# The queue order of an FNet and H3 kernel, taken from another machine model in the scheduler

## Chip, cores and metric

One core of a Trainium2 chip runs the whole program in one launch. The metric is the device time of one execution in microseconds (us), median over runs; less is better. The profile is of one further execution.

## What is computed

Two mixing layers are applied in turn, twice: an FNet layer (A) and an H3 layer (B). S = 2048 positions, D = 576 channels, float32.

```python
def _A_ref(x, dft_seq_re, dft_seq_im, dft_hid_re, dft_hid_im):
    a = jnp.einsum("bsd,ed->bse", x, dft_hid_re)
    b = jnp.einsum("bsd,ed->bse", x, dft_hid_im)
    return jnp.einsum("ts,bse->bte", dft_seq_re, a) - jnp.einsum("ts,bse->bte", dft_seq_im, b)

def _B_ref(q, k, v, shift_k, ssm_k, ssm_D):
    ...                      # k_shift: causal convolution of k with 4 taps
    kv = k_shift * v
    ...                      # y: causal convolution of kv with ssm_k over all 2048 positions, by FFT
    y = y + kv * ssm_D[None, None, :]
    return q * y

x = x + _A_ref(_layernorm(x), ...)
x = x + _B_ref(_layernorm(x), B_k, B_v, ...)
x = x + _A_ref(_layernorm(x), ...)
x = x + _B_ref(_layernorm(x), B_k, B_v, ...)
```

The factor y of layer B does not depend on x, so it is computed once and used in both B layers.

## The kernel before

Every float32 operand of a matmul is held as two float32r parts, a high and a low one, and a product takes three matmuls (high x high, high x low, low x high). `split` (L72, L73) makes the parts: ACT copies the high part, DVE subtracts it to get the low one. All matmuls are issued by the helper at L58.

**The trunk** is the first A layer: the sequence transform of the normalised x, then the hidden transform. `layer` (L251) runs 128 steps: 4 blocks of output positions (tb), for each the real and then the imaginary matrix (g), for each 16 steps k over the positions that are summed. Here a *trunk block* is one (tb, g), 16 steps, numbered 0 to 7. Step k loads one 128 x 512 tile of coefficients (`load_c`, L172; rings of three buffers, craw and cs), splits it, and runs 14 matmuls: 12 into four accumulators s0 to s3 and 2 into rm, which holds the last 64 channels. At the block's end `evac_u` splits the four accumulators into U, and `evac_r` does the same for rm:

```python
    def evac_r(g, ps):
        ...
        tmp = work()[lo:lo + REM, :NT]
        nc.scalar.activation(tmp, ps[NC][other:other + REM], AF.Copy)
        nc.vector.tensor_tensor(tmp, tmp, ps[NC][lo:lo + REM], OP.add)
        split(u[:, 0, :], u[:, 1, :], tmp)
```

Those are L216 to L224, with L222 on ACT and L223 on DVE. There is one buffer each for s0 to s3, rm and U. After both blocks of a tb the hidden transform `hidden` (L226) runs 8 pieces of 27 matmuls each (`bk<-w,mats` in the profile), one piece at a time between trunk steps, and the first of them need the weights from `load_w`.

**The branch** (`branch`, from L296) computes y of layer B with an FFT in three stages, written into the program between the trunk steps, with counts that set how many of its pieces stand ahead of which step (L538 to L546):

- The first stage (`f1_loads`, `f1_split`, `f1_products`; `bk<-f1r`): 32 units of 12 matmuls. A unit of v takes eight DVE operations (L347, L349, L350) for the 4 taps and the product with v. Results go to DRAM from ACT's queue (L364, L365).
- The middle stage (`mid_split`, `mid_forward`, `mid_inverse`; `bk<-mid`): 64 groups. A group reads one tile back from DRAM, splits it, runs 6 matmuls into two banks, copies (ACT, L399 to L402) and multiplies (DVE, L405 to L408), splits again, runs 3 matmuls into a third bank, and stores (L419, L420).
- The inverse stage (`i2_split`, `i2_products`; `bk<-i`): 16 pieces of 12 matmuls, which leave y in DRAM (yb).

The branch and the hidden transform share three PSUM banks (bk).

**The end of layer 1.** For each of 16 tiles, `get_x1` (L508) loads the result of the first A layer (xa) and yb, normalises and gates (`gated`, L474 and L475), stores, normalises again (`normed`, L148, L150), stores y for the second layer, and writes the split X tile (`to_x`, L155 to L158). The second A layer uses another algorithm (`strassen`) for three of its four tb and ends with 16 hidden tiles and gatings.

**Rings.** Scratch and landing buffers are slots cut out of a few large tiles, and a ring hands them out in the order in which the program is written. `work` (four slots, then three) serves the first and middle stage, the normalisations and evac_r alike; `land` (three or four) serves the loads of branch, weights, xa and yb; `res` (two) the x tiles. An operation that gets a slot waits until everything written earlier in the program is done with it.

**What sets the order.** The program is written as one sequence. A scheduler gives each of the five queues (TensorE, DVE, ACT, POOL, and SP, which issues most loads) its instructions in an order that it chooses: it runs the program on a model of the machine, and at each point takes, of the instructions that are ready there, the one that is earliest in the program. The order it finds is then fixed, and semaphore waits are put in. Loads of coefficients in the later part are held behind each other by `issue_after` (L126).

## Time and profile before

| | us |
|---|---|
| median of 3 runs | 1280.3 (1276.68 to 1282.56) |
| the profiled execution | 1286.63 |
| its span, first to last instruction | 1284.6 |
| granted TensorE clock, mean | 0.98 of full speed |

The span of the profiled execution falls into these parts. The times of the trunk blocks' ends are those of their last rm matmul.

| part | us from the start of the span |
|---|---|
| end of trunk blocks 0, 1, 2, 3 | 84.5, 166.5, 247.7, 360.3 |
| end of trunk blocks 4, 5, 6, 7 | 464.9, 543.1, 657.3, 718.8 |
| last matmul of the first stage of the branch | 218.5 |
| first gating of layer 1 (L475) | 674.3 |
| second layer's first rm matmul | 750.0 |
| last 16 hidden tiles | from about 1165 |

Busy time in some stretches of 40 us, us of 40:

| stretch | TensorE | DVE | ACT | GB/s |
|---|---|---|---|---|
| 0 to 40 | 29.39 | 26.60 | 24.69 | 300 |
| 200 to 240 | 36.26 | 20.52 | 25.57 | 231 |
| 440 to 480 | 38.51 | 34.72 | 34.89 | 150 |
| 720 to 760 | 28.78 | 28.93 | 12.43 | 187 |

In a line of the groups, after the shapes and the count come the busy time in us and the mean of one instruction in ns, then the idle time of the engine just before them and what ended most of it. In a line of the timeline stand the start, the duration, the engine and the line of the kernel, and in brackets the idle time before and what ended it. In the rows of tenths each digit is the busy share of one fortieth of the span, 32.1 us.

### The profile page before, as it was taken

Reading aid. Unit: us, or ns where it says so; the run is one execution under the profiler, and the core shown is the slowest. Engines: PE = TensorE matmul, PEld = TensorE weight load, DVE = VectorE, ACT = ScalarE, POOL = GpSimd, SP = SyncE. Lnnn points to the kernel's source line nnn. Section 1 sums busy time; section 2 is a strip of 40 time slices with the busy share of each in tenths; the row PEclk is TensorE's granted clock in tenths of the full one; section 3 lists DMA queues with packets and bytes.
Section 4 is the critical chain, followed back from the end, with each engine's and each line's share of the span. In section 5 each row is a group of like instructions: output and inputs, shape, how many; then the busy total and the mean of one; then the engine's idle time right before and its main releaser. Section 6 shows DMA issues by size and latency. Waiting matters only on the chain.

```text
span 1284.6 us, 18381 instructions
## 1 busy us (share of the span) xinstructions
PE 1210.3 (94%) x6320; PEld 1040.3 (81%) x6320; DVE 866.2 (67%) x1597; ACT 654.2 (51%) x1290; POOL 50.7 (4%) x68
## 2 busy tenths in 40 slices
PE   6799999799999999999999879899999999989998
PEld 5677888698889888789878768787878778779997
DVE  6788895737775697853358865565666657775764
ACT  5775675728865688854553332434443344451200
POOL 1100000000000000000002111000000000000111
PEclk9999999999999999999999989899999989999999
DMA  8968888635544555447878754774375467586642
GB/s 300 294 200 257 280 250 268 201 100 157 164 135 133 147 150 161 146 129 223 260 243 249 218 192 158 232 245 128 115 251 166 132 214 233 153 264 214 205 152 74
DMA packets 140367, 250.32 MB, mean 195 GB/s; under 512 B 15217, under 2 KB 39793, under 8 KB 140274
## 3 DMA queue, kind: packets, MB, share of 16 engines
q1 hardware_dynamic: 106290, 206.68, 52.5%
q10 hardware_dynamic: 33984, 42.48, 9.4%
q8 instruction: 49, 0.80, 0.3%
q14 instruction: 44, 0.36, 0.1%
HBM read 187.76 MB, written 61.34 MB: 194 GB/s over the span
## 4 chain that ended last, share of the span: by engine, by line
PE 53%; DMA 18%; DVE 11%; ACT 9%; issue 6%; POOL 1%; ACTq 0%; SPq 0%; POOLq 0%; DVEq 0%
PE s L58 27%; PE bk L58 23%; PE rm L58 4%; DMA flts<-vd 3%; DMA flts<-in_c_mat 3%; DVE mats L73 2%; DMA flts<-yb 2%; DMA flts<-in_x 2%; DMA t<-flts 1%; ACT mats L72 1%; DMA t<-f1f 1%; DMA flts<-xa 1%; DVE flts L408 1%; ACT flts L401 1%; DMA ud<-ph 1%
## 5 line engine op out<-in xcount | busy, mean ns | idle before, releaser
L58 PE MATMUL s<-mats 128*128 128x512 f32 x2292 | 583.2, 396 | 15.8 <-ACT mats L155 7.7
L58 PEld LDWEIGHTS s<-mats 128*128 128x128 f32 x2292 | 426.5, 190 | 103.1 <-ACT mats L155 10.0
L72 ACT ACTIVATE mats<-flts 128x512 fp32r<-128x512 f32 (+1 forms) x270 | 167.5, 626 | 180.3 <-PE rm L58 113.8
L73 DVE TENSOR_TENSOR mats<-flts,mats 128x512 fp32r<-128x512 f32 (+1 forms) x270 | 183.7, 686 | 81.8 <-ACT mats L72 80.0
L58 PE MATMUL bk<-w,mats 128*128 128x288 f32 x864 | 124.0, 299 | 4.8 <-DVE mats L73 3.0
L58 PEld LDWEIGHTS bk<-w,mats 128*128 128x128 f32 x864 | 119.9, 192 | 7.8 <-DVE mats L73 3.7
L58 PE MATMUL rm<-mats 128*128 128x512 f32 x338 | 107.0, 398 | 8.3 <-DVE flts L223 8.3
L58 PE MATMUL bk<-mid 128*128 128x288 f32 x576 | 97.6, 303 | 14.8 <-ACT mid L72 9.0
L58 PEld LDWEIGHTS bk<-mid 128*128 128x128 f32 x576 | 85.4, 189 | 30.8 <-ACT mid L72 12.4
L58 PE MATMUL s<-t,mats 128*128 128x512 f32 x384 | 99.1, 396 | 2.1 <-ACT ph L616 1.3
L72 ACT ACTIVATE mid<-flts 128x288 fp32r<-128x288 f32 (+1 forms) x128 | 71.7, 563 | 40.6 <-DVE flts L408 35.9
L58 PE MATMUL bk<-mats 128*128 128x288 f32 (+1 forms) x580 | 92.0, 304 | 0.0
L143 POOL TENSOR_TENSOR flts<-flts 128x1 f32<-128x1 f32 x56 | 43.2, 773 | 1199.4 <-DVE flts L142 1188.9
L58 PEld LDWEIGHTS s<-t,mats 128*128 128x128 f32 x384 | 73.1, 191 | 18.7 <-ACT ph L616 1.7
L72 ACT ACTIVATE t<-flts 128x512 fp32r<-128x512 f32 x78 | 48.6, 628 | 73.3 <-PE rm L58 19.4
L58 PEld LDWEIGHTS bk<-mats 128*128 128x128 f32 x580 | 82.3, 189 | 2.4
L73 DVE TENSOR_TENSOR mid<-flts,mid 128x576 fp32r<-128x576 f32 (+1 forms) x128 | 77.0, 606 | 9.2 <-ACT mid L72 5.3
L58 PEld LDWEIGHTS rm<-mats 128*128 128x128 f32 x338 | 64.2, 191 | 22.0 <-DVE flts L223 8.7
L73 DVE TENSOR_TENSOR t<-flts,t 128x512 fp32r<-128x512 f32 x78 | 53.3, 688 | 30.4 <-ACT t L72 30.1
L58 PE MATMUL bk<-f1r 128*128 128x288 f32 x384 | 63.8, 304 | 10.3 <-ACT f1r L72 7.0
L58 PEld LDWEIGHTS bk<-f1r 128*128 128x128 f32 x384 | 59.1, 194 | 17.1 <-ACT f1r L72 7.0
L238 DVE TENSOR_TENSOR flts<-flts,bk 128x288 f32<-128x288 f32 x56 | 25.2, 451 | 54.9 <-PE bk L58 54.6
(112 smaller groups left out, 1327.5 us busy)
## 6 DMA issues: line engine op xcount, KB each, us to landing
flts<-in_c_mat SPq DMA_DIRECT2D x84, 512.0 KB, 4.0
flts<-in_c_mat SPq DMA_DIRECT2D x160, 256.0 KB, 3.6
flts<-t SPq DMA_DIRECT2D x64, 288.0 KB, 2.9
t<-f1f ACTq DMA_DIRECT2D x42, 288.0 KB, 4.3
flts<-in_x SPq DMA_DIRECT2D x32, 288.0 KB, 4.0
vd<-flts ACTq DMA_DIRECT2D x64, 144.0 KB, 3.2
flts<-vd SPq DMA_DIRECT2D x32, 288.0 KB, 3.6
flts<-yb SPq DMA_DIRECT2D x32, 288.0 KB, 3.5
```

Of the source, the lines that this page charges most:

```text
L58: nc.tensor.matmul(ps, lhsT, rhs, start=first, stop=last, skip_group_check=more)
L72: nc.scalar.activation(h, src, AF.Copy)
L73: nc.vector.tensor_tensor(l, src, h.bitcast(F32), OP.subtract)
L143: nc.gpsimd.tensor_tensor(rs, ve, mhalf, OP.pow)
L238: nc.vector.tensor_tensor(xa[:, cs], r[:, cs], ps[:, :HD], OP.add)
L401: nc.scalar.activation(kk[lo, 1, :], pk[hi, :HD], AF.Copy)
L408: nc.vector.tensor_tensor(p1, p1, p2, OP.add)
```

## The change

The model of the machine on which the scheduler runs the program is exchanged: the default one for the scheduler's timeline model. The kernel function, its tiles, buffers and instructions stay as they are; only the order of each queue, and with it where the semaphore waits stand, comes out of another model.

```diff
     o = nc.dram_tensor("out_0", (P, J, D), F32, kind="ExternalOutput").ap()
-    with tile.TileContext(nc, auto_bufs=True) as tc:
+    with tile.TileContext(nc, auto_bufs=True, schedule_with_timeline_sim=True) as tc:
         fnet_h3_kernel(tc, **args, out=o)
```

Of the queues of the built program, 4367 of TensorE's 6322 instructions stand at another place than before (42 places on average over the queue, 261 at most), 1197 of DVE's 1599, 1187 of ACT's 1448, 433 of SP's 654, and 4 of POOL's 73.

## The prediction

> **What bounds the kernel now.** I read the page's shares and slices first, then the groups by line, the timeline of the one long stall, and stretches of the span.
>
> ```profile
> span 1284.6 us, 18381 instructions
> PE 1210.3 (94%) x6320; PEld 1040.3 (81%) x6320; DVE 866.2 (67%) x1597; ACT 654.2 (51%) x1290; POOL 50.7 (4%) x68
> PE   6799999799999999999999879899999999989998
> DVE  6788895737775697853358865565666657775764
> ACT  5775675728865688854553332434443344451200
> GB/s 300 294 200 257 280 250 268 201 100 157 164 135 133 147 150 161 146 129 223 260 243 249 218 192 158 232 245 128 115 251 166 132 214 233 153 264 214 205 152 74
> ```
>
> TensorE is the bound: 74 us of the span without it. The reader should see where its digits fall below 9: at the start, in slice 8 (about 225 to 255 us) and in slices 23, 24 and 26 (from 707 us). In between DVE and ACT are at 7 to 8 tenths, so there the branch (convolution) and the trunk (sequence transform) only just fit beside each other.
>
> ```profile
> L73 DVE TENSOR_TENSOR mid<-flts,mid 128x576 fp32r<-128x576 f32 (+1 forms) x128 | 77.0, 606 | 9.2 <-ACT mid L72 5.3
> L405 DVE TENSOR_TENSOR flts<-bk,flts 128x288 f32<-128x288 f32 x64 | 29.2, 456 | 30.3 <-ACT flts L400 30.2
> L140 DVE BATCH_NORM_STATS2 flts<-flts 128x6 f32<-128x288 f32 x104 | 44.4, 450 | 20.9 <-DMA flts<-xa 14.7 <-DMA flts<-in_x 4.9
> ...
> 674.33 0.81 DVE L475 SCALAR_TENSOR_TENSOR flts<-flts 128x576 f32<-128x576 f32 x1
> ...
> 747.59 0.81 DVE L475 SCALAR_TENSOR_TENSOR flts<-flts 128x576 f32<-128x576 f32 x1
> 748.13 0.59 ACT L222 ACTIVATE flts<-rm 64x512 f32<-64x512 f32 x1 [1.48 <-DMA y<-flts]
> 749.28 0.69 DVE L223 TENSOR_TENSOR flts<-flts,rm 64x512 f32<-64x512 f32 x1
> 750.03 1.65 PE L58 MATMUL rm<-mats 128*128 128x512 f32 x3 [8.25 <-DVE flts L223]
> ```
>
> The last four lines are the key. At the end of each trunk block evac_r (L222, L223) must empty the one rm bank before TensorE can go on with the next block's rm. Its scratch comes from the work ring, which hands out slots in program order, so it waits for the branch or normalising work written ahead of it, here for the store of a y. Whatever branch work is late at a block end, TensorE waits for there.
>
> Prices. One trunk step is 14 matmuls from 792.27 to 795.45 us, 0.227 each; 27 hidden matmuls take 3.55 us, 0.1315 each. One group of the mid stage (9 matmuls) costs DVE 2 x 0.606 + 0.456 + 0.459 + 0.450 + 0.451 = 3.03 us and ACT 2 x 0.563 + 1.62 (L399 to L402) + 0.41 = 3.15.
>
> **The change part by part.** No instruction is added or removed; each queue has the same ones, addresses and data as before. What differs is order, which the built program shows. On TensorE's queue trunk steps now run ahead and branch matmuls come later. Branch matmuls that stand ahead of the end of trunk block n, before and after: block 1, 240 and 153; block 2, 417 and 327; block 3 (mid alone), 210 and 132; block 4, 372 and 306; block 5, 534 and 462; block 6 (inverse stage), 156 and 72. The missing ones then stand in one stretch without trunk between a block's end and the next block's rm: 66, 57 + 39, 69, 63 and 63 in a row, where before the longest such stretch, but for the one joined to the hidden product, was 18.
>
> (a) Start. On SP's queue the fourth x load now stands behind six k_pad loads, two v and a second shift_k: 9.70 MB instead of 4.46. At the 297 GB/s of the first two slices it issues at 32.7 us, not 14.3; its X came 11.5 us after the issue (25.8), now 9.5 to 11.5 after, so about 43. From there to the sixteenth X DVE has 48.1 us of queued work (before 48.9, done in 56.2). End of block 0's X at 91 (DVE without a gap) to 99 (old pace), against 82.0. Fewer loads are left by then, so nearer the first: +10 (6 to 17).
>
> (b) Block 1. Between its evac_u and L223 DVE has 28 instructions, 20.6 us (8 L347 and 6 L349 at 0.752, 6 L73, 2 L350, the evacuations); TensorE has 38 x 0.227 + 84 x 0.1315 = 19.7 beside it. +2 (0 to 6, if ACT's 17 us alternate with it).
>
> (c) Block 2, the join with the hidden product. From the end of step 44 (where ACT may split the coefficients of step 47) TensorE has 42 x 0.227 + 141 x 0.1315 = 28.1 us to the 27th hidden matmul; ACT has 31.7 + 0.6 us up to the last weight split, and the store and reload between first and middle stage (4.3 + 2.9 us, rows of t) now have no trunk over them: 41 with the last split and matmuls. Before: 24.9 us elapsed for 17.4 of TensorE, 7.5 lost. 12.9 less 7.5 is +5 (-2 if the reload is hidden after all, +12 if chains add a fifth).
>
> (d) Blocks 3, 4, 5. DVE between evac_u and L223, block 3: 4 x 0.683 + 0.686 + 18 x 0.606 + 9 x 1.816 + 0.68 = 31.4 us; likewise 27.9 (15 and 8) and 30.9 (17 and 9). TensorE beside it: 38 trunk matmuls and 87, 75, 81 of the middle stage: 20.1, 18.5, 19.3. Left over 11.3, 9.4, 11.6; before these three ends lost 1.0, 0.3 and 2.2. So +29 if DVE runs without a gap. It won't: with three bk banks (two for a forward product, one for an inverse) a group goes TensorE 0.8, ACT 1.6, DVE 0.9, and only then are both banks free, some 3.5 us with hand-overs. Worst 4 us a group: +50. I take 3.5 us: 24 to 26 groups x 0.47 more, part of it beside the evacuations: +36.
>
> (e) End of layer 1 (block 7). The inverse stage is late by 84 matmuls at block 6, so the first gating (L475) ends only just before the last evac_u; before, 8 of 16 had. In both orders L223 stands behind the twelfth L475. DVE work from evac_u to L223 was 53 instructions, 23.4 us, and took 27 (722.9 to 750.0); it is now 151 instructions, 62.2 us (44 x 0.450, 23 x 0.205, 23 x 0.149, 11 x 2.74 for L474, L475, L148, L157, L158, and 4.1). Gatings went at (747.59 - 674.33) / 11 = 6.66 us each, a land ring of three: 11 of them are 73. TensorE's own work there is 18 us as before. 62 to 73 plus 1, less 27: +36 to +47, I take +41. What follows (X of steps 12 to 15) keeps its old distance.
>
> (f) Slow restarts. After 2.60 us idle twelve trunk matmuls took 4.51 us, otherwise 2.89; in 740 to 760 us the granted clock was 0.74. Six new long waits at 1.6 each, partly within the terms above: +4 (0 to 10).
>
> The Trainium skill (TensorE: Matmul & The Clock Gate, Part 1: The HAM clock gate) says that an idle window of about 3.4 us halves the clock, and about as long a busy one restores it. By it each long stall costs about 1.7 us of half speed and (f) would be 10, the sum +98; it also speaks for the second rival below. The trace agrees in kind, but here 2.60 us of idle time were enough.
>
> (g) Trunk steps run with fewer branch groups between them, so short waits inside blocks go. From 80 to 720 us TensorE was idle 24.5 us, about 12 of it not in the joins above: -6 (-12 to 0).
>
> From block 7's end on, TensorE's queue is nearly unchanged: 0.
>
> Sum: 10 + 2 + 5 + 36 + 41 + 4 - 6 = +92; ends 6 + 0 - 2 + 29 + 36 + 0 - 12 = +57 and 17 + 6 + 12 + 50 + 47 + 10 + 0 = +142. The profiled execution took 1286.6 us, span 1284.6 and 2.0 around it; with +92 it would take 1378.6. Its time is 6.3 over the median of the runs, 1280.3, so the median becomes **1372 us** (1337 to 1422).
>
> **Rivals.** *The middle backlog melts*: ACT and DVE get ahead inside the blocks, and only (e) stays: 1280.3 + 41 = 1321. For it: their idle share before the stretches; against it: df has two buffers, bk three banks, and the mid matmuls themselves are late in the queue.
>
> *Half clock through the stretches*: bursts of 1.2 us with gaps of 2 keep the clock low. The branch matmuls of (b) to (d), 84 + 96 + 27 + 87 + 75 + 81 = 450, at 0.1315 more add up to 59 us: about 1430. For it the 0.74 above; against it, that DVE and ACT pace those stretches and hide half of it.
>
> *Faster*: with the trunk ahead TensorE is never without a ready step, and the 24.5 us and the 11.2 us at block 7 (8.25 and 2.97) go: 1280.3 - 35.7 = 1245. It decides if L223 comes no later after evac_u than before at blocks 3, 4, 5 and 7. Against it are 23 to 27 us more DVE work ahead of it at each of the three, 39 at the last.
>
> *The order does not matter*: the queues meet again in the same waits, 1280. Against it: engines here start in queue order (the 8.25 us above was such a wait).
>
> **How the numbers follow.** My forecast 0.70, backlog melts 0.12, half clock 0.10, faster 0.05, no difference 0.03. About 0.5% (6 us) is what a measurement of this kernel tells from no change. Slower: 0.70 + 0.12 + 0.10 = 0.92; same 0.03; faster 0.05. The range takes in the first rival, 1318 to 1420, and leaves out the others.
>
> **What would show it.** Right: PE digits of 5 or less in slices near 140 to 170, 225 to 270, 360, 470, 550 and from 720 us; PE rm waiting for L223 for 30 us or more in total, once 40 or more; DVE and ACT busy sums unchanged; the fourth X after 38 us. Wrong: PE rm's wait for L223 near 8 us, or a mid group at 5 us or more in the stretches (then (d) was too small), or trunk steps longer than 3.2 us between them (a bound by loads that I count as nothing).

## The result, and the profile after

The kernel after takes 1394.0 us (median; 1390.9 to 1395.5), before 1280.3. The ratio is 1.0888, with a 95% interval of 1.0856 to 1.092: 9% slower, 113.7 us. The profiled executions took 1394.6 and 1286.6 us, their spans are 1392.8 and 1284.6, so they account for 108.2.

The page of after: the shares, and in 40 slices of 34.8 us the busy tenths of TensorE and the granted clock.

```profile
span 1392.8 us, 18367 instructions
...
PE 1243.4 (89%) x6320; PEld 1070.1 (77%) x6320; DVE 873.9 (63%) x1597; ACT 654.1 (47%) x1290; POOL 50.6 (4%) x68
...
PE   4889989599979989979999914989999999999998
...
PEclk9899999689969997979999956999999999999999
```

VectorE and ScalarE do what they did before (866.2 and 654.2 us). TensorE is busy for 33 us more with the same matmuls, so some run slower, and its share falls from 94 to 89%. Two holes stand out, slice 8 (244 to 279 us) and slices 24 and 25 (801 to 871); in slices 12, 16 and 18 (from 383, 522 and 592 us) TensorE still has 7 to 9 tenths, but its clock digit is 6 or 7.

What TensorE waits for in after: total in us, how many times, the longest.

```profile
PE rm L58 <- DVE flts L223: 48.2, 2, 46.9
PE bk L58 <- ACT mid L72: 35.6, 18, 7.3
PE s L58 <- ACT mats L155: 21.6, 10, 6.3
```

Before, these three were 8.3, 9.0 and 7.7 us. The first is nearly all one wait, the end of layer 1, seen in the timeline of after:

```profile
852.39 0.82 DVE L475 SCALAR_TENSOR_TENSOR flts<-flts 128x576 f32<-128x576 f32 x1
...
853.62 0.21 DVE L157 TENSOR_TENSOR mats<-flts,mats 128x64 fp32r<-128x64 f32 x1
...
854.60 0.59 ACT L222 ACTIVATE flts<-rm 64x512 f32<-64x512 f32 x1 [2.75 <-DVE mats L158]
...
855.26 0.69 DVE L223 TENSOR_TENSOR flts<-flts,rm 64x512 f32<-64x512 f32 x1
...
856.00 1.22 PE L58 MATMUL rm<-mats 128*128 128x512 f32 x2 [46.87 <-DVE flts L223]
```

It is the stall of before with the same instructions, 46.87 us where it was 8.25: L222 and L223 stand behind the twelfth gating (L475), and the gatings, which in before began at 674.3 us, began at 781.5.

The other places are read by windows. A *join* is the stretch from the last rm matmul of a trunk block to the first of the next. First the joins of blocks 1, 2, 3, 4, 5 and 7 in after; the columns are length, busy time (and count) of TensorE's matmuls, its weight loads, DVE, ACT and POOL, granted clock, share of the DMA engines, GB/s.

```profile
160.80:186.50 25.70, 22.11 (x121) 19.40 (x121) 18.79 (x27) 15.34 (x38) 0.00 (x0) 0.93 0.67 210
242.80:288.50 45.70, 28.18 (x124) 22.82 (x123) 23.52 (x41) 30.42 (x66) 0.00 (x0) 0.66 0.66 202
377.60:417.00 39.40, 30.21 (x124) 24.34 (x123) 28.72 (x58) 28.98 (x66) 0.00 (x0) 0.69 0.38 114
501.90:536.10 34.20, 25.70 (x112) 20.67 (x110) 26.15 (x53) 25.05 (x58) 0.00 (x0) 0.75 0.37 107
592.10:629.70 37.60, 28.66 (x117) 22.83 (x116) 27.60 (x56) 27.86 (x63) 0.00 (x0) 0.71 0.35 102
783.90:856.00 72.10, 20.79 (x108) 17.53 (x107) 52.01 (x149) 18.35 (x26) 16.13 (x23) 0.65 0.59 187
```

The same joins in before:

```profile
166.50:170.70 4.20, 4.20 (x25) 3.69 (x25) 4.11 (x7) 3.66 (x9) 0.00 (x0) 1.00 0.36 125
247.70:287.20 39.50, 36.47 (x253) 35.62 (x253) 18.01 (x35) 14.06 (x30) 0.00 (x0) 0.96 0.39 119
360.30:369.10 8.80, 8.37 (x49) 6.94 (x49) 8.09 (x16) 7.38 (x16) 0.00 (x0) 1.00 0.18 59
464.90:469.20 4.30, 4.30 (x22) 3.05 (x20) 4.27 (x9) 4.18 (x10) 0.00 (x0) 1.00 0.08 30
543.10:552.90 9.80, 7.90 (x49) 6.81 (x49) 9.05 (x19) 7.62 (x16) 0.00 (x0) 1.00 0.16 45
718.80:750.00 31.20, 20.01 (x108) 17.35 (x107) 24.51 (x61) 9.88 (x16) 4.66 (x7) 0.87 0.60 185
```

Before, joins 1, 3, 4 and 5 held 22 to 49 matmuls at full clock. After, they hold 112 to 124, most of them the branch's late ones with no trunk step beside them; at blocks 3, 4 and 5 TensorE, DVE and ACT are each busy for about three quarters of the time, taking turns, and the clock is 0.69 to 0.75 (0.93 at block 1, 0.66 at block 2).

To add this up I use one ledger for all kernels: the *loss* of a part is its elapsed time less its own matmuls at 0.227 us (512 wide) and 0.1315 us (288 wide), the prediction's prices. It holds idle time and matmuls slower than their price alike. "In blocks" is the sum within blocks 1 to 7. A matmul on a border can count on either side, so the rows are good to some tenths.

| loss, us | before | after |
|---|---|---|
| block 0 with its join | 26.7 | 38.2 |
| in blocks 1 to 7 | 39.7 | 11.7 |
| joins 1, 2 | -0.1, 5.2 | 6.5, 29.5 |
| joins 3, 4, 5 | 1.2, 0.4, 2.3 | 19.8, 16.2, 18.8 |
| joins 6, 7 | -0.1, 13.6 | -0.1, 54.5 |
| all behind block 7's join | 36.1 | 38.3 |

So the trunk loses less inside its blocks (28.0 us less), and 122.7 us more at its joins: it runs ahead of the branch and then waits for it.

### The profile page after: what moved, and what is told of

It is laid out like the page before. It is cut to its first block, busy times and chain, and to the rows that moved or that the text cites. A ratio compares the mean times of both kernels' runs of the same rounds, so it can differ in the third digit from the quotient of the medians.

```text
span 1392.8 us, 18367 instructions
## 1 busy us (share of the span) xinstructions
PE 1243.4 (89%) x6320; PEld 1070.1 (77%) x6320; DVE 873.9 (63%) x1597; ACT 654.1 (47%) x1290; POOL 50.6 (4%) x68
## 4 chain that ended last, share of the span: by engine, by line
PE 68%; DMA 14%; DVE 7%; ACT 7%; issue 3%; SPq 0%; POOL 0%; ACTq 0%; POOLq 0%; DVEq 0%
PE s L58 39%; PE bk L58 24%; PE rm L58 6%; DMA flts<-in_c_mat 3%; DMA y<-flts 3%; DVE mats L73 1%; DMA flts<-xa 1%; ACT mid L72 1%; DMA ph<-ud 1%; DMA xa<-flts 1%; DMA flts<-in_f1c 1%; DMA t<-flts 1%; DMA flts<-yb 1%; DMA flts<-in_x 1%; ACT flts L150 1%
## 5 line engine op out<-in xcount | busy, mean ns | idle before, releaser
L58 PE MATMUL s<-mats 128*128 128x512 f32 x2292 | 596.6, 398 | 27.6 <-ACT mats L155 21.6
L58 PE MATMUL bk<-mid 128*128 128x288 f32 x576 | 129.8, 355 | 42.9 <-ACT mid L72 35.6
L58 PEld LDWEIGHTS bk<-mid 128*128 128x128 f32 x576 | 107.3, 229 | 65.2 <-ACT mid L72 42.1
L58 PE MATMUL rm<-mats 128*128 128x512 f32 x338 | 111.1, 412 | 48.3 <-DVE flts L223 48.2
L72 ACT ACTIVATE mid<-flts 128x576 fp32r<-128x576 f32 (+1 forms) x128 | 70.6, 561 | 57.4 <-DVE flts L408 38.8
```

The lines of the kernel that those rows point to most:

```text
L58: nc.tensor.matmul(ps, lhsT, rhs, start=first, stop=last, skip_group_check=more)
L72: nc.scalar.activation(h, src, AF.Copy)
```

## The experiments

All kernels but one (c2) start from after. They were run in four groups, each beside the kernel before on the same chip, whose medians there were 1283.6 (h1 to h4), 1276.6 (c1, c2, s1), 1282.2 (h5, s2, h6) and 1277.3 us (m1). Where the source grows, its line numbers move by a few.

### Holding the trunk behind the branch

```diff
     def mm(ps, lhsT, rhs, first, last, more=False):
-        nc.tensor.matmul(ps, lhsT, rhs, start=first, stop=last, skip_group_check=more)
+        behind = who[0] == "trunk" and len(branch_mm) >= LAG
+        with tc.issue_after(branch_mm[-LAG]) if behind else ExitStack():
+            i = nc.tensor.matmul(ps, lhsT, rhs, start=first, stop=last, skip_group_check=more).ins
+        if who[0] == "branch":
+            branch_mm.append(i)
...
+            who[0] = "trunk" if blocks == TB and True else ""
             for dc in range(NC):
```

LAG is 12, and the condition `True` (all steps) is `F1_END < n <= MID_END` for the middle stage, `n > MID_END` with LAG 18 for the inverse stage and `n <= F1_END` for the first; `who` is set back behind a step, and to "branch" while the branch runs on.

All steps:

> The queues of after, but every trunk matmul has to stand behind the branch matmul that was written out 12 places before it, so that TensorE's queue can't run the trunk ahead of the branch. Theory (the loss is made where a trunk block waits for evac_r, whose ring slot comes free only when the late branch gets there): the joins of blocks 1 to 5 and 7 go back to what they lose before (+6.6, +24.3, +50.9 and +40.9 us come off), the 28 us of in-block waits return, the start stays +9.9: 1394 - 123 + 28 = about 1299 us, 1288 to 1315. Rival (the order of the other engines and of the loads makes the loss, and TensorE's order only shows it): 1370 or more. Rival (the slow clock of its own makes the stretches, not the wait for the slot): the mid matmuls stay at a mean of 355 ns and blocks 3 to 5 keep at least 30 us of their 55.

Middle stage:

> The same hold for the trunk matmuls of the middle stage's steps alone. Theory: blocks 3, 4 and 5 lose 2 to 5 us at their joins in place of 16 to 20 (51 us come off), block 2 loses 5 to 20 in place of 29.5, some 5 to 15 us of in-block waits return, block 7 keeps its 54: 1335 to 1355 us, likeliest 1345. Rival (the other engines' order): within 10 us of 1394.

Inverse stage:

> The same hold (18 places) for the trunk matmuls of the inverse stage's steps alone. Theory: the join of block 7 goes from 54 us to 10 to 18 us, nothing else moves: 1350 to 1360 us. Rival (the inverse stage's backlog of loads, splits and stores runs after the trunk in any order of the matmuls, since 12 rounds of it are still to be done): 1385 to 1394, with the 40 us shown as waits inside block 7 or after it.

First stage:

> The same hold for the trunk matmuls of the first stage's steps alone. Theory: the joins of blocks 1 and 2 lose 0 to 2 and 5 to 10 us in place of 6.5 and 29.5, about 10 of the 28 us of in-block waits return, blocks 3 to 7 stay: 1368 to 1385 us. Rival (block 2's 29.5 us are hidden's chunk loads and the store-and-reload round trip at the stage's change, not the first stage's lateness): the join of block 2 stays over 20 us and the time within 8 us of 1394.

Measured, with the loss at joins 1, 2, 3 to 5 together and 7:

| | median, us | ratio to before | in blocks 1 to 7 | 1 | 2 | 3 to 5 | 7 |
|---|---|---|---|---|---|---|---|
| after | 1394.0 | 1.0888 [1.0856, 1.092] | 11.7 | 6.5 | 29.5 | 54.8 | 54.5 |
| h1, all | 1332.1 | 1.0382 [1.0346, 1.0417] | 78.4 | 0.9 | 4.4 | 3.1 | 8.3 |
| h2, middle | 1351.8 | 1.0537 [1.0504, 1.057] | 50.0 | 6.5 | 0.1 | 1.8 | 51.2 |
| h3, inverse | 1381.0 | 1.0775 [1.0741, 1.081] | 31.4 | 6.4 | 29.9 | 57.0 | 18.3 |
| h4, first | 1382.4 | 1.0777 [1.0736, 1.0818] | 12.6 | 1.8 | 21.9 | 57.5 | 53.4 |

h1: all joins together lose 18.0 us where after loses 145.2 and before 22.5, with no instruction changed and all queues still ordered by the new model. So the trunk's lead makes the joins' loss, and the rival's 1370 or more did not come. But the hold did not move TensorE's queue alone. In the order of starts in the traces (instructions matched by operation, tile and shape), those of DVE stand on average 6.0 places away from their place in before in after, and 1.8 in h1; those of ACT 7.2 and 1.9. How much of the loss passes through the order of DVE and ACT is not separated here. The rival of a clock which is slow by itself falls: the mid matmuls are back at a mean of 304 ns (355 in after, 303 in before). But 1332 us is above the 1288 to 1315 expected: inside the blocks 78.4 us are lost, 39 more than in before. I had counted on the 28 us of before coming back, and nothing for the hold.

h2: in its range. Blocks 3, 4 and 5 lose 0.4, 0.7 and 0.7 us at their joins. Block 2's loss only moves (27.4 us inside it, 0.1 at its join, where after has 1.8 and 29.5). In all 38 us come back inside the blocks, where 5 to 15 were expected.

h3: a miss. Join 7 falls by 36 us to 18, at the edge of what was expected, but block 6 loses 15.1 us (2.0 in after) and block 7 6.3 (0.8). The rival comes closer: 13 us are gained, not 41. Its waits of TensorE from 628 to 844 us:

```profile
PE rm L62 <- DVE flts L229: 12.9, 1, 12.9
PE bk L62 <- ACT i L78: 10.4, 5, 5.3
```

(L229 is L223 here.) Held, TensorE waits for the first pieces of the inverse stage as well, since the middle stage ahead of it is as late as in after (join 5 loses 21.0 us).

h4: 1382.4, in the theory's range, but join 2 stays at 21.9 us, as the rival said: only 7.6 of its 29.5 us go when the trunk is held behind the first stage.

### Cutting the tie between evac_r and the branch

```diff
-        tmp = work()[lo:lo + REM, :NT]
+        tmp = ring["craw"]()[lo:lo + REM]
```

> After, but evac_r takes its scratch row from the ring of C chunks, which only the trunk uses, and not from the work ring, which the branch shares; the scheduler then makes its order anew. Theory (what the late branch does to the trunk passes through that one ring slot): evac_r no longer waits for the branch at any join, the waits for DVE L223 fall from 48 us to under 10, and the joins of blocks 1, 3, 5 and 7 lose 0 to 6 us each in place of 6.5, 19.8, 18.8 and 54.5; part of it comes back where hidden must be done (blocks 2, 4 and 6) and as in-block waits: 1300 to 1365 us, likeliest 1335. Rival (a branch that is late costs the same wherever it meets the trunk): 1380 or more, with the loss at blocks 2, 4 and 6 or behind block 7.

1349.7 us, ratio 1.0565 [1.0518, 1.0612], in the range. The waits of TensorE:

```profile
PE s L58 <- ACT mats L155: 35.7, 16, 6.3
PE bk L58 <- ACT mid L72: 23.4, 11, 7.9
PE bk L58 <- ACT f1r L72: 9.0, 1, 9.0
```

The wait for L223 is gone but for 0.8 us (48.2 before this edit), and no join loses more than 0.6 us. What is left shows the other half: blocks 3 and 7 now lose 38.6 and 39.7 us inside (1.2 and 0.8 in after), in the first mostly to waits for the middle stage (16.3 us) and slow matmuls around them, and 59.2 us are lost behind block 7 (38.3), where X tiles for the second layer come late (the first row). At blocks 2, 4 and 6, where it was expected, nothing comes back. So both theories hold in part: without the slot's tie 44 of the 114 us go (41 by the ratios, each to before on its own chip), and the rest is paid at other meetings of branch and trunk. The 44 are those of the cut with the order that the scheduler then found, not of the cut in the order of after.

The same edit in the kernel before:

> The same edit of evac_r in the kernel before, whose queues are in the order of before. Theory: the one join of before that loses much (block 7, 13.6 us) loses 2 to 5, the others stay: 1268 to 1276 us. Rival (behind block 7 layer 2 needs the last rounds of the inverse stage anyway): 1278 to 1284, the loss shown behind the join.

1274.7 us, ratio 0.9979 [0.9959, 0.9999]. Block 7's join loses 4.6 us in place of 13.6, as the theory said. Yet the medians show only 2 us of these 9, with an interval that just leaves out no change; the spans of the two profiled executions differ by 8.8 (1275.8 and 1284.6), and that of before was one of the longer ones. It is the fastest kernel of this study, by less than its measurement can hold for certain.

### The start

```diff
-            nc.sync.dma_start(t, bass.AP(tensor=k_pad.tensor, ...))
+            with tc.issue_after(x_load[min(3 + 2 * i, max(x_load))]):
+                nc.sync.dma_start(t, bass.AP(tensor=k_pad.tensor, ...))
```

> After, but each load of k_pad stands behind a load of x on SP's queue (the first behind the fourth x load, as in before). Theory for the start: block 0 loses 27 to 31 us in place of 36.8, the rest stays: 1384 to 1390 us. Rival (what makes the start late are the other loads and DVE's order, since the fourth x load still stands behind loads of v and C): block 0 keeps 35 us or more, 1392 to 1400.

SP's queue at the start of after, loads of x and k_pad (start of the issue; x2 are two issues):

```profile
3.84 0.43 SPq L496 DMA_DIRECT2D flts<-in_x  x1
...
6.80 0.33 SPq L496 DMA_DIRECT2D flts<-in_x  x1
...
7.18 0.46 SPq L313 DMA_DIRECT2D f1f<-in_k_pad  x1
...
18.94 1.75 SPq L313 DMA_DIRECT2D f1f<-in_k_pad  x2
...
21.85 1.00 SPq L496 DMA_DIRECT2D flts<-in_x  x2
```

The loads of x in s1:

```profile
6.71 0.33 SPq L497 DMA_DIRECT2D flts<-in_x  x1
...
14.81 0.33 SPq L497 DMA_DIRECT2D flts<-in_x  x1
```

The fourth x load goes from 21.9 to 14.8 us (14.3 in before), the high part of the sixteenth X is made at 84.3 us in place of 90.4 (80.1). Block 0 with its join loses 32.1 us, after 38.2, before 26.7: half of the late start is these loads. The time, 1382.0 us (1.0812 [1.0771, 1.0852]), is below the range expected (before took 3.7 us less on this chip than in the first runs): by the ledger 6 us come from the start, 5 from block 7 and what follows it, 2 from the rest.

Loads of v behind those of x as well:

```diff
-            nc.sync.dma_start(r, (ssm_k if src else v)[:, j, :])
+            with ExitStack() if src else tc.issue_after(x_load[min(3 + 2 * j, max(x_load))]):
+                nc.sync.dma_start(r, (ssm_k if src else v)[:, j, :])
```

> s1_xfirst, with the loads of v behind loads of x as well. Theory (the start is late because loads of the branch stand ahead of loads of x): block 0 loses 26 to 29 us in place of 32.2, 1374 to 1380 us. Rival (the rest of the start is the order of the norms on VectorE and ScalarE, since in s1 the fourth x load is issued at 14.8 us, as in before at 14.3, and its norm is still done 3 us later): block 0 stays at 31 to 33, 1379 to 1385.

A miss of both: 1389.9 us (1.0842 [1.0815, 1.0868]), and block 0 with its join loses 36.7. The fourth x load is at 15.8 us, yet from the seventh on the X tiles (their high parts) come in pairs (42.0 and 42.6, 52.0 and 52.5, 72.1 and 73.6 us), and TensorE waits 4.4 us for one of them at 85 us. The other half of the start stays open.

### What the hold itself costs, and whether the terms add

```diff
-            who[0] = "trunk" if blocks == TB and True else ""
+            who[0] = "trunk" if blocks == TB and not (F1_END < n <= F1_END + 3 or MID_END < n <= MID_END + 3) else ""
```

> h1_hold_all, but the trunk is not held in the three steps after each change of the branch's stage (first to middle, middle to inverse), where the branch waits for its store to come back as a load. h1 still lost 21.5 us in block 2 with its join and 19.8 in block 6, against 12.4 and 6.5 in before. Theory (that rest is the price of the hold: TensorE stands idle through the round trip and runs at half clock behind it): blocks 2 and 6 lose 8 to 18 us less together: 1313 to 1324 us. Rival (the stage changes themselves cost that in the order of the other engines): within 5 us of 1332.

1321.2 us, 1.0295 [1.0275, 1.0315]: the time is in the range, but the edit did not test the reason. Blocks 2 and 6 with their joins lose 37.3 us where h1 loses 41.3, four less and not 8 to 18. The round trip is still bare; TensorE's timeline in h5, from the first stage's last matmuls to the middle stage's first:

```profile
237.32 0.67 PE L62 MATMUL bk<-f1r 128*128 128x288 f32 x3 [1.47 <-ACT f1f L372]
244.92 0.85 PE L62 MATMUL bk<-mid 128*128 128x288 f32 x2 [6.94 <-ACT mid L78]
245.57 5.32 PE L62 MATMUL s<-mats 128*128 128x512 f32 x12
...
255.30 4.16 PE L62 MATMUL s<-mats 128*128 128x512 f32 x12
...
260.68 2.88 PE L62 MATMUL s<-mats 128*128 128x512 f32 x12
```

6.94 us without work, and then two trunk steps whose twelve matmuls take 5.32 and 4.16 us in place of 2.88. Counted through the trunk, these are steps 44 and 45, which h5 holds again. The three that it frees (41 to 43) ran ahead of the first stage's last 18 matmuls and left nothing to cover the round trip; at the second change it is the same (97 to 99 ran ahead, step 100 stands behind the first inverse pieces). So whether covering the round trip pays was not tried. In before no wait for the middle stage in this block is longer than 2.8 us.

With the k_pad edit of s1 and the craw edit of c1 on top:

> h5, with the k_pad loads behind the x loads (as in s1) and evac_r's scratch row from the C ring (as in c1). Theory (the terms are separate and add): h5 less 4 to 6 us at the start and 3 to 6 at the join of block 7: 1303 to 1314 us. Rival (with TensorE's order held, the scratch ring no longer matters): less than 2 us from it, and the gain is the start alone.

1320.9 us, 1.0304 [1.027, 1.0339]: no gain over h5, where the terms add up to 7 to 12. Its profiled execution has both gains (block 0 with its join 33.1 for 39.6, join 7 3.6 for 8.2), and loses part again at blocks 1 and 2 and their joins (30.3 for 23.3). Its runs spread from 1317.7 to 1327.5, so a few us can't be told. The terms do not simply add.

### The chain of a middle group

```diff
             for ps, o in ((pk, HD), (px, 0)):
+                for _ in range(3 if ps is pk else 0):
+                    mm(ps[:, :HD], mc[:, 0, :], df[0][:, o:o + HD], True, False, True)
                 mm(ps[:, :HD], mc[:, 0, :], df[0][:, o:o + HD], True, False)
```

> After, with three matmuls more in each of the 64 middle groups (the first product of the group's first bank is done four times, the next start overwrites it; the result stays). Disputed: in the stretches of blocks 3, 4 and 5 a group takes 3.93 us where 3.5 was forecast, with its nine matmuls at half clock (2.5 to 2.8 us; 1.2 at full). Theory (TensorE at half clock is a link of the group's chain, so what it does longer the group does longer): three matmuls at half clock, some 0.8 us, come onto each group of a stretch, 4.5 to 4.8 us; with 25 us of matmuls in all at full clock and some 27 groups in the stretches 1418 to 1432 us. Rival (ScalarE and VectorE bound the group, TensorE waits for them in any case): the groups stay at 3.9 to 4.1 us, some 10 us of the 25 vanish in the stretches, 1402 to 1412 us.

TensorE in block 3's stretch of after:

```profile
394.18 2.53 PE L58 MATMUL bk<-mid 128*128 128x288 f32 x9 [1.93 <-ACT mid L72]
399.16 2.72 PE L58 MATMUL bk<-mid 128*128 128x288 f32 x9 [2.45 <-ACT mid L72]
...
410.69 2.53 PE L58 MATMUL bk<-mid 128*128 128x288 f32 x9 [1.50 <-ACT mid L72]
```

The same stretch in m1:

```profile
401.14 3.67 PE L58 MATMUL bk<-mid 128*128 128x288 f32 x12 [0.62 <-ACT flts L404]
405.46 3.50 PE L58 MATMUL bk<-mid 128*128 128x288 f32 x12 [0.65 <-ACT mid L72]
411.04 1.87 PE L58 MATMUL bk<-mid 128*128 128x288 f32 x12 [2.07 <-ACT mid L72]
```

From one group's first copy (L399) to the next, after takes 3.93, 3.80 and 3.90 us in the stretches of blocks 3, 4 and 5, m1 4.24, 3.96 and 4.46. The first one or two groups of each stretch are left out; they take longer (4.5 to 8.3 us in after). In the last, where the clock of m1 is 0.54 (615.5 to 644 us), half a microsecond of the 0.8 arrives; in block 3's, where the added work brings the clock to 0.69 (0.58 in after) and twelve matmuls once take 1.87 us, less. So TensorE is a link of the chain, and 0.16 to 0.56 us of the added 0.8 reach the group: between the two theories. The time, 1408.0 us (1.1038 [1.0992, 1.1084]), is in the rival's range, but does not decide: 25.2 us of matmuls were added and the loss fell by 14.3, mostly 7 at block 7, 5 at block 4's join and 4 at block 2's, where the order made anew stands a little otherwise.

## Why the prediction was right, and which steps were not

The forecast was 1372 us and a range of 1318 to 1420; measured 1394.0. The mechanism was the one named: the trunk runs ahead, the branch is late, and TensorE pays at the joins, through evac_r's slot or through the branch matmuls that stand before the next rm. h1 shows the first part (undo the lead and the joins go back to 18 us), c1 the second (cut the slot, and in the order found then the joins go to nothing, the waits for L223 from 48 us to 0.8). How near the sum came is in part luck: two terms were right, four lay outside their own ranges. By the forecast's terms, in the ledger:

| term | forecast | measured | |
|---|---|---|---|
| (a) start | +10 (6 to 17) | +9.9 in block 0, +1.6 at its join | right; s1: half of it is k_pad |
| (b) block 1's join | +2 (0 to 6) | +6.6 | too small |
| (c) block 2's join | +5 (-2 to 12) | +24.3 | mis-sized |
| (d) joins 3, 4, 5 | +36 (29 to 50) | +50.9 | just past its far end |
| (e) join 7 | +41 (36 to 47) | +40.9 | right |
| (f) slow restarts | +4 (0 to 10) | inside (b) to (e) | the clock's part was larger |
| (g) waits in blocks | -6 (-12 to 0) | -28.0 | mis-sized |
| rest | 0 | +2.2 | |
| sum | +92 | +108.2 | |

(a): the mechanism stood, one size did not. The fourth x load went out at 21.9 us, not 32.7: until then 7.5 MB had moved at 343 GB/s, and the forecast let it wait for all 9.70 MB at 297. Its X was there at 37.0, not about 43, since it came 15.1 us after the issue and not 9.5 to 11.5. Later norms gave the difference back, and the sixteenth X is 10.3 us late, as forecast.

(c) is, beside (g), the term that was furthest off. I had 41 us from the end of step 44 to the 27th hidden matmul; it took 57.6. TensorE in after, behind block 2's last trunk step:

```profile
248.32 4.88 PE L58 MATMUL bk<-f1r 128*128 128x288 f32 x27 [0.36 <-ACT f1f L364]
260.48 2.12 PE L58 MATMUL bk<-mid 128*128 128x288 f32 x6 [7.28 <-ACT mid L72]
265.15 0.85 PE L58 MATMUL bk<-mid 128*128 128x288 f32 x2 [2.55 <-ACT mid L72]
...
271.81 2.48 PE L58 MATMUL bk<-mid 128*128 128x288 f32 x7 [2.99 <-ACT mid L72]
...
282.14 5.33 PE L58 MATMUL bk<-w,mats 128*128 128x288 f32 x22
```

The store and the reload were costed at 7.2 us, and TensorE's wait across them is 7.28, with the split of the tile in it. What was left out is that the matmuls on both sides of it are slow: 22 hidden matmuls take 5.33 us, 2.9 at the price of the full clock. In the join's window above TensorE is busy for 28.2 us with matmuls that are worth 16.2. That would be 12 of the 16.6 us missed, if all of it lies on the path; that was not tried by itself. h4 adds that holding the trunk behind the first stage brings back only 7.6 us.

(d): the chain of a group, 3.5 us in the forecast, took 3.8 to 3.9, as a group's nine matmuls took 2.5 to 2.8 us, not 1.2. m1 shows TensorE in the chain. Some 0.4 us for the 24 to 26 groups counted are 10 of the 15 us missed; the first groups of each stretch took longer still.

(e): from the start of evac_u's first low part to the next rm 73.7 us passed (782.3 to 856.0), where 62 to 73 and 1 were forecast. It went by the gatings' pace (70.8 us from the first L475 to the twelfth), not by DVE's work, which is 52.0 us of the join. But it is not all the price of this one place: h3 takes 36 us off the join, and 20 of them turn up in and around blocks 6 and 7.

(g) was sized by TensorE's idle time alone (24.5 us, 12 of it in blocks). Both halves of that fell short. The trace of before has 18.8 us of idle time in blocks 1 to 7, after 0.5: that is 18.3 of the 28.0 us. The rest are matmuls that take longer than their price, and hardly by the clock, which is 0.97 to 1.00 in each of these blocks, before and after; why they do is not shown. This error and those of (b), (c) and (d), +43 forecast and +81.8 measured, went against each other; the sum was off by 16 us and its terms by more. The median was off by 22: the forecast also took off the 6.3 us by which the profiled execution of before lay over its median, and that of after lay only 0.6 over.

Of the rivals, the melting backlog (1321) is out: joins 3 to 5 lose 54.8 us. The half clock (1430) was real in the stretches and not in the sum: in the six joins shown TensorE is busy for 155.6 us with matmuls that are worth 109.4, 46 us longer; how much of that ACT and DVE would have taken in any case is not shown. "Faster" had one thing right, the waits inside blocks do go, and its condition failed at every block it named.

Of the signs to look for, the wait of rm for L223 (48.2 us, once 46.9) and the unchanged sums of DVE and ACT came. The fourth X came at 37.0, just short of the 38 named. The TensorE digits of 5 or less came only at two of the places; at 360, 470 and 550 us they are 7 to 9, as slow matmuls count as busy, and the clock row shows them. Of the signs of being wrong none came: a group takes under 5 us on average even with the first ones of a stretch, and TensorE is idle for 0.5 us in blocks 1 to 7, so no trunk step waits for loads there. The wait at blocks 3, 4 and 5 is not booked under rm either but under mid: the next rm stands in TensorE's queue behind the late branch matmuls, which were put there while it could not go.

Open: between h5 (1321) and before (1282) remain some 39 us. By the ledger 13 are in block 0 with its join, 18 in blocks 2 and 6 at the changes of the branch's stage, 7 in blocks 3, 4 and 5. Why the start keeps its second half, and whether covering the round trips would bring the 18, was not settled. Nor was what the order of DVE and ACT alone does.

## What to carry to other kernels

When only the order of queues changes, compare for each rare join (a single bank, a scratch slot that rings hand out in program order) how much of the slower stream stands ahead of it: work that ran ahead gained 28 us inside its blocks here and paid 123 where the streams meet. A ledger of elapsed time less priced matmuls, part by part, finds this faster than idle times do, since slow matmuls hide in busy time. And before a long wait is put down to one semaphore, cut that one: here 44 of 114 us went with it, and the lateness behind it cost the rest at other places. And when an edit goes through a scheduler, look at where each instruction landed before reading the time: in h5 the steps set free were not those that stood behind the wait.

## What the runs showed of the hardware

The granted clock falls to half and stays there with gaps shorter than the 2.60 us of the forecast. In block 3's stretch of after it was 1.00 from 388.5 to 392.9 us and 0.50 from 393 to 416.5. It fell within a gap of 1.93 us (before the matmuls at 394.18), behind gaps of 0.83 and 0.48, and none later was over 2.45. The Trainium skill (TensorE: Matmul & The Clock Gate, HAM oscillation) names idle gaps over about 3.4 us as what brings the clock down; none here was that long. Its Part 1 adds that a busy window of about 3.4 us restores the clock; behind 4.20 and 2.23 us of matmuls with 0.22 us between them (402.5 to 409.2 us) the next nine still took 2.53 us. The trace counts these as busy, but TensorE's weight loads waited five times in them, for 0.20 to 0.56 us, so whether that was such a busy window is not shown. And more work can run faster: in m1, with three more matmuls in each group, the clock in that stretch was 0.69, and twelve matmuls once took 1.87 us where nine had taken 2.53.
